# One decode step on one core: K and V loaded per head and batch in 6 KB runs, in place of both batches of a head in 12 KB runs

## The chip, the core and the metric

The kernel runs on one core of a Trainium2 chip. The core has five engines with an instruction stream each: TensorE (PE, matrix products; its weight loads are shown apart as PEld), VectorE (DVE), ScalarE (ACT), GpSimd (POOL) and SyncE (SP). Loads go from HBM to SBUF, the on-chip memory of 128 partitions, through 16 DMA engines; here SP issues every load. The metric is the device time of one execution in microseconds (us), the median of several runs.

## The reference

One token for each of two batches passes an attention block and a gated feed-forward block. The attention reads the last 2048 of 8192 cached positions of 32 heads, each 192 wide; all data are bfloat16.

```python
B, Sq, D = 2, 1, 640
Hq, Hkv, Sk, Dh = 32, 32, 8192, 192
W = min(4096, max(256, Sk // 4))                      # 2048
q = (x @ wq).reshape(B, Sq, Hq, Dh).transpose(0, 2, 1, 3)
k = k_cache[:, :, Sk - W:, :]
v = v_cache[:, :, Sk - W:, :]
p = softmax(einsum("bhqd,bhkd->bhqk", q, k) * Dh ** -0.5)
o = einsum("bhqk,bhkd->bhqd", p, v).transpose(0, 2, 1, 3).reshape(B, Sq, Hq * Dh) @ wo

h = x + A(layernorm(x))
h2 = h + (gelu(n @ w_gate) * (n @ w_up)) @ w_down     # n = layernorm(h)
```

K and V of the window are 2 x 32 x 2048 x 192 x 2 bytes each, 100.7 MB together; the weights add 21.6 MB.

## The kernel before

**Order.** The program is written once, operation by operation, through `P.op`, which notes what each operation reads (`R`), writes (`W`) and shares (`X`) and works out the semaphore waits. Each engine then runs its own operations in the order of writing. The heads are taken two at a time in 16 groups (`NG`), both batches together, so a group has four pairs of head and batch.

**The ring.** All loads go into one buffer, `ring`, of 110,592 bytes in each partition, at places handed out one after the other; where a load doesn't fit up to the end, it starts at 0 again. `load` queues a load, and `pump` issues queued loads in order on SP (L261). A load is put down only after the work that last read any earlier load in its place has been written (`done`), and its instruction waits for that work. Overlap is followed in steps of 256 bytes (`GRAN`). The loads' order: K of group 0, the first quarter of wq, K of group 1; then for each group K of the next group (and every fourth time a quarter of wq ahead of it), V of this group, and the group's rows of wo; at the end w_gate, w_up and three thirds of w_down. A load signals one of 32 semaphores in turn.

**K and V.** `kv_src` gives one head of both batches as 128 rows: row 2i is positions 32i to 32i+31 of batch 0, and row 2i+1 the same of batch 1. So one load puts 128 runs of 12,288 bytes into 128 partitions, batches on alternate partitions; there are 32 loads of K and 32 of V, 1536 KB each.

**Work on a group.** PE turns K over in blocks of 128x128 four-byte words (L427, 24 blocks a load, into four banks `tps`), and ACT (L436) and DVE (L439) copy the results into `ktr`, 1024 columns at a time. A four-byte word is a pair of neighbouring bf16 values, and since partitions alternate between batches, one kind of value lies at every fourth element of `ktr`. `q_stationary` (L468) makes the query columns with a `mask`; `scores` (L489) makes the scores of the four pairs in 24 products; `softmax` takes the maximum (L494 to L500) and the exponential (L502). The exponential writes every value twice, 1024 columns, since each of the columns goes to both batches' partitions. `e_columns` (L512) brings the exponentials into columns with eight small products, and a masked product on DVE with `bmask` (L316, as one of many) puts each into the columns of its own batch in `ering`. `pv` (L527) multiplies with V, 32 products a load. `o_columns` (L539, L541) and `oproj` (L556) of the group before make the output projection and add it to `hT`; this frees that group's wo.

**Order in a group's turn** g, on PE: first half of the transposes of group g+1; `e_columns(g)`; `o_columns(g-1)`; every fourth time the next query rows (L447); second half of the transposes; `oproj(g-1)`; `q_stationary(g+1)`; `pv(g)` for the first head; `scores(g+1)`; `pv(g)` for the second head; `softmax(g+1)`.

**The end.** After group 15: its output projection, the second layer norm, the gate and up products (L606), the activation, the down products (L629), the sum into `yT`, and the store (L637).

Of the kernel before, what the change touches and what calls it, by code (L numbers as in the profile page):

```python
# [143 lines left out]
KTP = 4  # L144
# [5 lines left out]
def bass_sequential_preLN__sliding_block_cached__geglu_ffn__decode_kernel(  # L150
# [11 lines left out]
):  # L162
    rep = 2
    with ExitStack() as ctx:
# [6 lines left out]
        def sb(name, shape, dt):  # L171
            return ctx.enter_context(nc.sbuf_tensor(name, shape, dt))
# [5 lines left out]
        ktr = sb("ktr", [128, KTP, 3, 2048], BF16)  # L178
# [10 lines left out]
        bmask = sb("bmask", [128, 2], F32)  # L189
        sel16 = sb("sel16", [128, 16], BF16)  # L190
# [27 lines left out]
        eexp = sb("eexp", [128, 1024], BF16)  # L218
        ering = sb("ering", [128, 2, 2, 32, 32], BF16)
# [48 lines left out]
        def kv_src(cache, q):  # L268

            return cache[:, q, SKT - WIN:, :].rearrange("b (i t) d -> i b (t d)", t=32)  # L270

        def load_k(g):
            for q in (2 * g, 2 * g + 1):
                load(("k", q), 2 * 32 * DH, kv_src(A_k_cache, q), lambda v: v)

        def load_v(g):
            for q in (2 * g, 2 * g + 1):
                load(("v", q), 2 * 32 * DH, kv_src(A_v_cache, q), lambda v: v)
# [55 lines left out]
        pool(lambda e: e.iota(ei[:, :], pattern=[[256, 3], [1, 2]], base=0, channel_multiplier=2), W=["ei"])  # L334
        pool(lambda e: e.memset(ering[:, :, :, :, :].rearrange("p a b c d -> p (a b c d)").bitcast(I32), 0), W=[("er", 0), ("er", 1)])
# [60 lines left out]
        dve(ts(oh_b[:, :], cf[:, 2, 31:33], pf[:, 5:6], ALU.is_equal, 0.5, ALU.mult), R=["cf2", "pf5"], W=["oh_b"])  # L396
        dve(ts(sel[:, :], cf[:, 0, 0:32:16], pf[:, 1:2], ALU.is_equal), R=["cf0", "pf1"], W=["sel"])
        dve(lambda e: e.tensor_copy(ef[:, :], ei[:, :]), R=["ei"], W=["ef"])
        for r in range(5):
            dve(ts(ge[:, :, r], ef[:, :], 192.0 * r, ALU.is_ge), R=["ef"], W=[("ge", r)])  # L400
        dve(tt(mask[:, :, :], ge[:, :, 0:4], ge[:, :, 1:5], ALU.subtract), R=[("ge", r) for r in range(5)], W=["mask"])

        dve(lambda e: e.tensor_copy(sel16[:, :].rearrange("p (j m) -> p j m", m=4),
                                    identf[:, :].rearrange("p (j m) -> p j m", m=32)[:, :, 0:4]), R=["identf"], W=["sel16"])

        dve(ts(pti[:, 0:1], pi[:, :], 1, ALU.bitwise_and), R=["pi", "pf1"], W=["pti0"])
        dve(lambda e: e.tensor_copy(pf[:, 6:7], pti[:, 0:1]), R=["pti0"], W=["pf6"])
        dve(ts(bmask[:, :], cf[:, 0, 0:2], pf[:, 6:7], ALU.is_equal), R=["cf0", "pf6"], W=["bmask"])
        mask_toks = ["mask"]

# [3 lines left out]
        def transposes(q):  # L414

            kk, ktoks = where["k", q]
            kv = kk.bitcast(F32)
            slot = q % KTP
            for bank in range(6):
                c, half = bank // 2, bank % 2  # L420
                bi = tb_count[0] % 4
                tb_count[0] += 1

                def fn(e, c=c, half=half, bi=bi):
                    for u in range(4):
                        off = 384 * (4 * half + u) + 128 * c
                        ins = e.transpose(tps[bi][:, 128 * u:128 * (u + 1)], kv[:, off:off + 128], identf[:, :])  # L427
                    return ins

                pe(fn, R=ktoks + ["identf"], X=[("t", bi)])  # L430
                if bank == 5:
                    done(("k", q))
                bv = tps[bi][:, :].bitcast(BF16)
                dst = ktr[:, slot, c, 1024 * half:1024 * (half + 1)]
                if bank in (2, 5) or (bank == 3 and q % 2 == 0):
                    act(lambda e, dst=dst, bv=bv: e.activation(out=dst, in_=bv, func=ACT.Copy),  # L436
                        W=[("kt", slot, bank)], X=[("t", bi)])
                else:
                    dve(lambda e, dst=dst, bv=bv: e.tensor_copy(dst, bv), W=[("kt", slot, bank)], X=[("t", bi)])  # L439
# [19 lines left out]
        def q_stationary(g):  # L459
            p0 = 32 * (g % 4)  # L460
            qx = qrow[p0:p0 + 2, (g // 4) % 2, :, 0:rep, :].rearrange("p h r d -> p h (r d)")

            def fn(e):
                for h in range(2):
                    for k in range(6):
                        col = 12 * h + 2 * k
                        o = 256 * (k // 2) % DH + k % 2
                        ins = e.matmul(m1[:, col:col + 2], lhsT=qx[:, h, o:o + 255:2],  # L468
                                       rhs=identb[p0:p0 + 2, p0:p0 + 2], start=True, stop=True, tile_position=(p0, 0))
                return ins  # L470

            pe(fn, R=[("qrow", (g // 4) % 2), "identb"], X=["m1"])
            for h in range(2):
                for b in range(2):
                    j = 2 * h + b
                    src = m1[:, 12 * h + b:12 * h + 12:2].unsqueeze(2).to_broadcast([128, 6, 4])
                    dve(tt(rq[:, g % 2, j, :, 0:4], src, mask[:, :, :], ALU.mult), R=mask_toks,
                        W=[("rq", g % 2)] if j == 0 else [("rq", g % 2, j)], X=["m1"])
# [4 lines left out]
        def scores(g):  # L483
            def fn(e):
                for k in range(6):
                    for j in range(4):
                        b = j % 2
                        r = ktr[:, (2 * g + j // 2) % KTP, k // 2, 2 * b + k % 2:2048:4]
                        ins = e.matmul(sps[32 * j:32 * (j + 1), :], lhsT=rq[:, g % 2, j, k, :], rhs=r, start=(k == 0),  # L489
                                       stop=(k == 5), tile_position=(0, 32 * j))  # L490
                return ins

            pe(fn, R=rq_toks(g) + [("kt", (2 * g + h) % KTP, x) for h in range(2) for x in range(6)], X=["s"])
            dve(lambda e: e.tensor_reduce(out=mx[:, :], in_=sps[:, :], axis=AX.X, op=ALU.max), W=["mx"], X=["s"])  # L494
            dve(ts(mrhs[:, :], oh_k[:, :], mx[:, 0:1], ALU.mult), R=["oh_k", "mx"], W=["mrhs"])

        def softmax(g):
# [4 lines left out]
            act(lambda e: e.activation(out=eexp[:, :].rearrange("p (x d) -> p x d", d=2),  # L502
                                       in_=sps[:, :].unsqueeze(2).to_broadcast([128, 512, 2]), func=ACT.Exp, bias=nm[:, 0:1], scale=1.0,
# [3 lines left out]
        def e_columns(g):  # L507

            def fn(e):
                for u in range(8):  # L510
                    o = m2[:, 0:128].rearrange("p (j t) -> p j t", t=32)[:, :, 4 * u:4 * u + 4]
                    ins = e.matmul(o, lhsT=eexp[:, 128 * u:128 * (u + 1)], rhs=sel16[:, :], start=True, stop=True)  # L512
                return ins

            pe(fn, R=["eexp", "sel16"], X=["m2"])
            src = m2[:, 0:128].rearrange("p (h b t) -> p h t b", h=2, b=2)
            dst = ering[:, g % 2, :, :, 0:32:16]
            dve(tt(dst, src, bmask[:, :].unsqueeze(1).unsqueeze(1).to_broadcast([128, 2, 32, 2]), ALU.mult), R=["bmask"],
                W=[("er", g % 2)], X=["m2"])

        def pv(g, h):
            vv, vtoks = where["v", 2 * g + h]

            def fn(e):
                for t in range(32):
                    r = t % 4
                    ins = e.matmul(ops_[32 * r:32 * (r + 1), 192 * h:192 * (h + 1)], lhsT=ering[:, g % 2, h, t, :],  # L527
                                   rhs=vv[:, DH * t:DH * (t + 1)], start=(h == 0 and t < 4), stop=(h == 1 and t >= 28),
                                   tile_position=(0, 32 * r), skip_group_check=True)
                return ins  # L530

            pe(fn, R=[("er", g % 2)] + vtoks, X=["o"])
            done(("v", 2 * g + h))
            if h == 1:
                act(lambda e: e.activation(out=osb[:, :], in_=ops_[:, 0:384], func=ACT.Copy), W=["osb"], X=["o"])  # L535
# [31 lines left out]
        transposes(0)  # L567
        transposes(1)
# [4 lines left out]
        for g in range(NG):  # L573
            nxt = g + 1 < NG
            if nxt:
                transposes(2 * g + 2)
            e_columns(g)
            if g > 0:
                o_columns(g - 1)
            if nxt and (g + 1) % 4 == 0:  # L580
                q_rows((g + 1) // 4)
            if nxt:
                transposes(2 * g + 3)
            if g > 0:
                oproj(g - 1)
            if nxt:
                q_stationary(g + 1)
            pv(g, 0)
            if nxt:
                scores(g + 1)  # L590
            pv(g, 1)
# [105 lines left out]
```

## Time and profile before

| | us |
|---|---|
| median of three runs | 305.15 (304.78 to 305.48) |
| the profiled execution | 305.48 |
| its span, first to last instruction | 303.6 |

| in the profiled execution | busy us | share of the span |
|---|---|---|
| PE, products | 235.6 | 78% |
| PEld, weight loads | 190.1 | 63% |
| DVE | 130.5 | 43% |
| ACT | 112.2 | 37% |
| load queue, mean of 16 DMA engines | | 96.9% |

The span is cut into 40 equal slices in the page, and each digit tells the busy share of a slice in tenths. "q1" is the queue of the loads that SP issues; its packets are the single contiguous runs and the small signals at a load's end. In a row of waits the columns are the engine and line that waited, what it waited for, the total, the number of times, and the longest, in us. A row of a group of instructions has the line, engine, operation, tiles and shapes, the count, the busy time in us and the mean of one in ns, and then the idle time ahead of it with what ended it. HBM was read at 403 GB/s over the span.

### The profile page before, as it was taken

How to read it: one execution, taken by the hardware profiler on the slowest of the kernel's cores; microseconds unless marked ns; L12 is line 12 of the kernel's file. 1: busy time of each engine (PE TensorE's matmuls, PEld its weight loads, DVE VectorE, ACT ScalarE, POOL GpSimd, SP SyncE). 2: the span in 40 equal slices, each digit the busy share in tenths (PEclk: the TensorE clock that was granted, in tenths of full speed). 3: DMA queues.
4: the chain of work that ended last, by engine and by line, in shares of the span. 5: the costliest groups of instructions: out<-in, count | busy, mean ns of one | idle time of the engine just before them, and what ended most of it. 6: DMA issues, size and time to landing. Idle time of an engine off the chain costs nothing.

```text
span 303.6 us, 7058 instructions
## 1 busy us (share of the span) xinstructions
PE 235.6 (78%) x3169; PEld 190.1 (63%) x3169; DVE 130.5 (43%) x360; ACT 112.2 (37%) x138; POOL 3.2 (1%) x9
## 2 busy tenths in 40 slices
PE   2878798962999988791898979692799889796762
PEld 1737394932868675771867676671785858575662
DVE  5837263720345364341446454351252736453120
ACT  2336343630425263522336353432243644442000
POOL 4000000000000000000000000000000000000000
PEclk9999979995798899798799999798579999998555
DMA  6999999999999999999999999999999999999980
GB/s 240 412 435 414 427 426 420 428 399 427 425 422 423 426 421 421 427 399 428 421 428 426 421 418 426 421 407 420 433 419 426 421 421 417 429 419 424 417 308 27
DMA packets 16323, 122.76 MB, mean 404 GB/s; under 512 B 1698, under 2 KB 3236, under 8 KB 7844
## 3 DMA queue, kind: packets, MB, share of 16 engines
q1 hardware_dynamic: 16292, 122.30, 96.9%
q8 instruction: 25, 0.41, 0.6%
q14 instruction: 6, 0.05, 0.0%
HBM read 122.29 MB, written 0.00 MB: 403 GB/s over the span
## 4 chain that ended last, share of the span: by engine, by line
DMA 57%; PE 31%; SPq 5%; DVE 3%; ACT 1%; issue 1%
DMA ring<-in_A_k_cache_dram 49%; PE tps L427 19%; DMA ring<-in_B_w_down_dram 8%; SPq L261 5%; PE m L541 3%; PE sps L489 3%; PE m L556 2%; PE ops L527 1%; ACT eexp L502 1%; PE m L447 1%; PE m L468 1%; PE m L539 1%; DVE mx L494 1%; DVE ktr L439 1%; PE m L512 1%
## 5 line engine op out<-in xcount | busy, mean ns | idle before, releaser
L427 PE MATMUL tps<-identf,ring 128*128 128x128 f32 x768 | 109.5, 305 | 37.4 <-DMA ring<-in_A_k_cache_dram 33.2
L427 PEld LDWEIGHTS tps<-identf,ring 128*128 128x128 f32 x768 | 101.1, 161 | 42.4 <-DMA ring<-in_A_k_cache_dram 34.0
L436 ACT ACTIVATE ktr<-tps 128x1024 bf16<-128x1024 bf16 x80 | 79.6, 1023 | 77.4 <-PE tps L427 77.4
L439 DVE COPY ktr<-tps 128x1024 bf16<-128x1024 bf16 x112 | 73.7, 688 | 47.3 <-PE tps L427 45.4
L489 PE MATMUL sps<-ktr,rq 128*32 128x512 bf16 x384 | 46.5, 631 | 0.7 <-DVE rq L316 0.5
L535 ACT ACTIVATE osb<-ops 128x384 f32<-128x384 f32 x16 | 7.9, 491 | 71.5 <-PE ops L527 71.5
L494 DVE TENSOR_REDUCE mx<-sps 128x1 f32<-128x512 f32 x16 | 11.1, 692 | 49.4 <-PE sps L489 49.4
L527 PEld LDWEIGHTS ops<-ring,ering 128*32 128x32 bf16 x1024 | 22.9, 101 | 10.5 <-issue 9.0
L527 PE MATMUL ops<-ring,ering 128*32 128x192 bf16 x1024 | 28.5, 255 | 0.2 <-DMA ring<-in_A_v_cache_dram 0.2
L489 PEld LDWEIGHTS sps<-ktr,rq 128*32 128x32 bf16 x384 | 10.9, 108 | 21.9 <-issue 21.0
L502 ACT ACTIVATE eexp<-sps,nm 128x1024 bf16<-128x1024 f32 x16 | 17.8, 1114 | 12.7 <-DVE nm L500 12.7
L541 PE MATMUL m<-sel,osb 128*128 128x2 f32 x96 | 19.4, 318 | 0.0
L541 PEld LDWEIGHTS m<-sel,osb 128*128 128x128 f32 x96 | 18.6, 269 | 0.0
L556 PEld LDWEIGHTS m<-ot,ring 128*128 128x128 bf16 x240 | 11.8, 129 | 1.1 <-DVE ot L316 1.1
L312 DVE TENSOR_SCALAR zrhs<-oh_b,zr 128x2 f32<-128x2 f32 x16 | 3.7, 229 | 20.4 <-ACT eexp L502 20.4
L556 PE MATMUL m<-ot,ring 128*128 128x2 bf16 x240 | 11.6, 177 | 0.9 <-DVE ot L316 0.9
L316 DVE TENSOR_TENSOR ering<-m,bmask 128x128 bf16<-128x128 f32 x16 | 11.3, 709 | 1.9 <-PE m L512 1.3
L498 PEld LDWEIGHTS m<-mrhs,pm 128*128 128x128 f32 x32 | 4.8, 188 | 11.5 <-DVE mrhs L312 11.5
L498 PE MATMUL m<-mrhs,pm 128*128 128x4 f32 x32 | 6.2, 263 | 7.1 <-DVE mrhs L312 7.1
L316 DVE TENSOR_TENSOR rq<-m,mask 128x24 bf16<-128x24 f32 x64 | 7.2, 175 | 9.6 <-PE m L468 9.6
L468 PE MATMUL m<-identb,qrow 2*128 2x2 bf16 x192 | 7.2, 159 | 4.6 <-DVE hT L316 3.7
L468 PEld LDWEIGHTS m<-identb,qrow 2*128 2x128 bf16 x192 | 5.8, 92 | 6.3 <-DVE hT L316 4.8
(84 smaller groups left out, 85.4 us busy)
## 6 DMA issues: line engine op xcount, KB each, us to landing
ring<-in_A_k_cache_dram SPq DMA_DIRECT2D x32, 1536.0 KB, 24.2
ring<-in_A_v_cache_dram SPq DMA_DIRECT2D x32, 1536.0 KB, 24.7
ring<-in_A_wq_dram SPq DMA_DIRECT2D x4, 1920.0 KB, 23.7
ring<-in_A_wo_dram SPq DMA_DIRECT2D x16, 480.0 KB, 19.7
ring<-in_B_w_gate_dram SPq DMA_DIRECT2D x1, 1920.0 KB, 27.4
ring<-in_B_w_up_dram SPq DMA_DIRECT2D x1, 1920.0 KB, 22.4
ring<-in_B_w_down_dram SPq DMA_DIRECT2D x3, 640.0 KB, 23.7
xrow<-in_A_x_dram SPq DMA_DIRECT2D x1, 2.5 KB
```

Source lines behind the costliest of these rows:

```text
L261: P.op("sp", lambda e, v=v, src=src: e.dma_start(v, src), W=toks + [("sem", i % NSEM)], dma=f"d{i % NSEM}")
L316: return lambda e: e.tensor_tensor(out=out, in0=a, in1=b, op=op)
L427: ins = e.transpose(tps[bi][:, 128 * u:128 * (u + 1)], kv[:, off:off + 128], identf[:, :])
L436: act(lambda e, dst=dst, bv=bv: e.activation(out=dst, in_=bv, func=ACT.Copy), W=[("kt", slot, bank)], X=[("t", bi)])
L439: dve(lambda e, dst=dst, bv=bv: e.tensor_copy(dst, bv), W=[("kt", slot, bank)], X=[("t", bi)])
L468: ins = e.matmul(m1[:, col:col + 2], lhsT=qx[:, h, o:o + 255:2], rhs=identb[p0:p0 + 2, p0:p0 + 2], start=True, stop=True, tile_position=(p ...
L489: ins = e.matmul(sps[32 * j:32 * (j + 1), :], lhsT=rq[:, g % 2, j, k, :], rhs=r, start=(k == 0), stop=(k == 5), tile_position=(0, 32 * j))
L494: dve(lambda e: e.tensor_reduce(out=mx[:, :], in_=sps[:, :], axis=AX.X, op=ALU.max), W=["mx"], X=["s"])
L502: act(lambda e: e.activation(out=eexp[:, :].rearrange("p (x d) -> p x d", d=2), in_=sps[:, :].unsqueeze(2).to_broadcast([128, 512, 2]), fu ...
L527: ins = e.matmul(ops_[32 * r:32 * (r + 1), 192 * h:192 * (h + 1)], lhsT=ering[:, g % 2, h, t, :], rhs=vv[:, DH * t:DH * (t + 1)], start=(h ...
L541: ins = e.matmul(m1[:, 32 + 2 * kk:34 + 2 * kk], lhsT=osb[:, kk:384:3], rhs=sel[:, :], start=True, stop=True)
L556: ins = e.matmul(m1[:, 48 + 2 * c:50 + 2 * c], lhsT=wo[:, kk, c:D:NC5], rhs=ot[:, kk, :], start=(kk == 0 and c == 0), stop=(kk == 2), skip ...
```

## The change

K and V are loaded for each head and batch alone. `kv_src(cache, n)` with n = 2 head + batch gives 128 rows of 16 positions, 6,144 bytes each and next to each other in HBM; there are 64 loads of K and 64 of V, 768 KB each. The places in the ring are in turn half as large, and come free one by one. The order of the bytes is otherwise kept. What follows from it in the work:

- `transposes(n)` handles one pair of head and batch in three banks of four blocks; a turn has four of them, and the other steps stand between them: one; `e_columns`; one; `o_columns`, query rows; one; `oproj`; one; `q_stationary`. `ktr` has 8 places of 1024 columns in place of 4 of 2048, and the scores read every second element.
- The exponential writes 512 columns. `e_columns` makes four 128x128 transposes in place of eight products, and a plain copy on DVE of 64 columns takes the place of the masked product; `bmask` and `sel16` go, and the factor 0.5 in `oh_b` with them. `ering` holds, for each pair, stationary columns shifted by batch.
- `pv(g, j)` runs for each of the four pairs, 16 products each: two ahead of the scores of the next group, two behind.
- A constant `LAYOUT`, set to "f32", chooses between two ways of turning K over; only the first is in the program that is built, and it is left out below where it has no effect.

```diff
-KTP = 4
+KTS = 8
...
-        ktr = sb("ktr", [128, KTP, 3, 2048], BF16)
+        ktr = sb("ktr", [128, KTS, 3, 1024], BF16)
...
-        eexp = sb("eexp", [128, 1024], BF16)
-        ering = sb("ering", [128, 2, 2, 32, 32], BF16)
+        eexp = sb("eexp", [128, 512], BF16)
+        ESTR = 528
+        ering = sb("ering", [128, 2, 4 * ESTR], BF16)
...
-        def kv_src(cache, q):
-
-            return cache[:, q, SKT - WIN:, :].rearrange("b (i t) d -> i b (t d)", t=32)
+        def kv_src(cache, n):
+            h, b = n // 2, n % 2
+            return cache[b, h, SKT - WIN:, :].rearrange("(p t) d -> p (t d)", p=128)
 
         def load_k(g):
-            for q in (2 * g, 2 * g + 1):
-                load(("k", q), 2 * 32 * DH, kv_src(A_k_cache, q), lambda v: v)
+            for n in range(4 * g, 4 * g + 4):
+                load(("k", n), 2 * T * DH, kv_src(A_k_cache, n), lambda v: v)
...
-        def transposes(q):
...
-            for bank in range(6):
-                c, half = bank // 2, bank % 2
+        def transposes(n):
+            for c in range(3):
...
-                        off = 384 * (4 * half + u) + 128 * c
+                            off = 384 * u + 128 * c
...
-                if bank == 5:
-                    done(("k", q))
+                if c == 2:
+                    done(("k", n))
...
-                if bank in (2, 5) or (bank == 3 and q % 2 == 0):
+                if c == 2 or (c == 1 and n % 4 == 1):
...
-                        r = ktr[:, (2 * g + j // 2) % KTP, k // 2, 2 * b + k % 2:2048:4]
+                            r = ktr[:, n % KTS, k // 2, :].rearrange("p (s e) -> p e s", e=2)[:, k % 2, :]
...
-            act(lambda e: e.activation(out=eexp[:, :].rearrange("p (x d) -> p x d", d=2),
-                                       in_=sps[:, :].unsqueeze(2).to_broadcast([128, 512, 2]), func=ACT.Exp, bias=nm[:, 0:1], scale=1.0,
+            act(lambda e: e.activation(out=eexp[:, :], in_=sps[:, :], func=ACT.Exp, bias=nm[:, 0:1], scale=1.0,
...
-                for u in range(8):
-                    o = m2[:, 0:128].rearrange("p (j t) -> p j t", t=32)[:, :, 4 * u:4 * u + 4]
-                    ins = e.matmul(o, lhsT=eexp[:, 128 * u:128 * (u + 1)], rhs=sel16[:, :], start=True, stop=True)
+                for cc in range(4):
+                    ins = e.transpose(ev[:, 128 * cc:128 * (cc + 1)], eexp[:, 128 * cc:128 * (cc + 1)], identb[:, :])
...
-            dve(tt(dst, src, bmask[:, :].unsqueeze(1).unsqueeze(1).to_broadcast([128, 2, 32, 2]), ALU.mult), R=["bmask"],
-                W=[("er", g % 2)], X=["m2"])
+            dve(lambda e: e.tensor_copy(dst, src), W=[("er", g % 2)], X=["m2"])
...
-        def pv(g, h):
-            vv, vtoks = where["v", 2 * g + h]
+        def pv(g, j):
+            n = 4 * g + j
...
-            done(("v", 2 * g + h))
-            if h == 1:
+            done(("v", n))
+            if j == 3:
...
             if nxt:
-                transposes(2 * g + 2)
+                transposes(4 * g + 4)
             e_columns(g)
+            if nxt:
+                transposes(4 * g + 5)
             if g > 0:
                 o_columns(g - 1)
             if nxt and (g + 1) % 4 == 0:
                 q_rows((g + 1) // 4)
             if nxt:
-                transposes(2 * g + 3)
+                transposes(4 * g + 6)
             if g > 0:
                 oproj(g - 1)
             if nxt:
+                transposes(4 * g + 7)
                 q_stationary(g + 1)
             pv(g, 0)
+            pv(g, 1)
             if nxt:
                 scores(g + 1)
-            pv(g, 1)
+            pv(g, 2)
+            pv(g, 3)
```

## The prediction

> **What bounds the kernel now.** I read the page's slices and DMA queue first, then stretches of single load kinds, then SP's waits, then the last 30 us. The page:
>
> ```profile
> span 303.6 us, 7058 instructions
> ...
> PE 235.6 (78%) x3169; PEld 190.1 (63%) x3169; DVE 130.5 (43%) x360; ACT 112.2 (37%) x138; POOL 3.2 (1%) x9
> ...
> DMA  6999999999999999999999999999999999999980
> ...
> q1 hardware_dynamic: 16292, 122.30, 96.9%
> ```
>
> The load queue keeps its 16 engines busy for 96.9% of the span: 0.969 x 303.6 = 294.2 us on each engine. The remaining 9.4 us are the start (the trace's first packet begins at 1.7 us) and the end (its last load packet ends at 297.4 us, 6.2 us ahead of the end of the span); between 8 and 281 us the packet records show only 1.3 us of idle time per engine. The busiest compute engine, PE, has 78%, and most of its idle time is a wait for K. So DMA time is the time.
>
> Next, the rate by size of packet. A packet is one contiguous run into one partition. In these stretches (DMA share and GB/s are the last two columns) the records hold 12 KB packets of K and V alone in the first three, 92% wq packets of 3072 B in the fourth, and in the last the down-projection's 1280 B packets:
>
> ```profile
> core 0: us, PE busy (x) PEld busy (x) DVE busy (x) ACT busy (x) POOL busy (x), PEclk, DMA share, GB/s
> 72.00:79.00 7.00, 4.72 (x22) 4.72 (x23) 1.54 (x3) 1.86 (x2) 0.00 (x0) 0.50 1.00 425
> 120.00:127.00 7.00, 4.31 (x45) 3.99 (x34) 2.55 (x6) 2.91 (x5) 0.00 (x0) 0.80 1.00 423
> ...
> 212.00:219.00 7.00, 4.37 (x21) 4.37 (x22) 1.38 (x2) 1.51 (x2) 0.00 (x0) 0.50 1.00 421
> ...
> 64.50:67.00 2.50, 1.74 (x42) 1.04 (x34) 1.08 (x3) 0.62 (x2) 0.00 (x0) 1.00 1.02 398
> ...
> 294.00:297.00 3.00, 2.27 (x56) 2.06 (x53) 0.51 (x3) 0.00 (x0) 0.00 (x0) 0.50 0.57 201
> ```
>
> The reader is to see that the queue is full in the first four rows and yet slower with small packets. The last row shows a share of 0.57: about half of the engines are done (in the records they end at 292 to 293 us), the others at 296 to 297. The end hangs on the later half.
>
> Then whether the queue ever runs dry:
>
> ```profile
> ring<-in_A_k_cache_dram SPq DMA_DIRECT2D x32, 1536.0 KB, 24.2
> ring<-in_A_v_cache_dram SPq DMA_DIRECT2D x32, 1536.0 KB, 24.7
> ```
> ```profile
> SPq L261 <- PE m L556: 140.1, 13, 20.8
> SPq L261 <- PE ops L527: 24.4, 12, 3.1
> ```
>
> A K load moves in 3.7 us (1.57 MB at 423 GB/s) but lands 24 us after its issue: it stands in line. SP's waits for ring places (the output projection's at L556 above all) are long, yet the bytes issued less the bytes landed never fall under 2.8 MB after the start (at 155.4 us), which is 6.6 us of transfer.
>
> **The change, part by part.**
>
> *Packets (L261).* Bytes stay the same. K and V go from 64 loads of 128 packets of 12,288 B to 128 loads of 128 packets of 6,144 B: 8192 packets become 16,384, or 512 more on each engine. The trace before has no 6 KB packet, so I bound its cost. From the stretches: 16 x 12288 / 423 = 464.8 ns a packet; the fourth row has a mean packet of 3,122 B, 16 x 3122 / 398 = 125.5 ns. The slope is (464.8 - 125.5) / 9166 = 0.0370 ns per byte, and 125.5 - 3122 x 0.0370 leaves 9.9 ns for every packet whatever its size. The records agree: mean durations of 57, 124, 151, 464 and 577 ns at 1280, 3072, 3840, 12,288 and 15,360 B (the slowest 0.5% left out) lie on one line. Split by rank, the quicker 7/16 of the packets of each size (as seven engines' worth) leave 7.8 ns and the slower 9/16 leave 11.8. The low end is the quick group, 512 x 7.8 = 4.0 us; the high end takes the slow tenth of the 3840 and 12,288 B packets (156 and 469 ns: 241.4 ns at 6144 B, 482.8 - 469 = 13.8 ns), 7.1 us. The later engines set the end, so I choose between all engines' 9.9 and the slow group's 11.8: 10.8 ns, 512 x 10.8 = **5.5 us**.
>
> *Completions.* 64 more loads each end in one 4-byte packet per engine, 9 ns in the records: 64 x 9 = **0.6 us**. Bounds: 0, if it lies beside the next packet, and 1.5 us, if each also takes as much idle time as the records show per load between packets (the 1.3 us above over 91 loads, 14 ns).
>
> *Issues on SP.* 64 more of some 0.55 to 0.6 us are 38 us, on an engine that waits over 200 us for places and for the end; each one feeds 786 KB, 1.9 us of transfer. Cost on the path **0**, hidden by the queued loads. One limit shows: some issues last up to 7.0 us in place of 0.54, when about 75 to 85 packets per engine stand unfinished. With 6 KB packets that limit is reached at half the bytes, but 75 x 0.238 = 18 us are then still queued, so SP is late and DMA is not. If this cover were gone, one 0.6 us issue per load would still be under 1.9 us.
>
> *Ring.* 12,288 is two times 6144, so all offsets, wraps and the order of the loads stay. Places come free in halves, and the output projection (which frees its weights) comes after three of four K pieces in place of all: some 1.9 us sooner. This can only lengthen the queue. **0**.
>
> *Waits on PE.* The transposes now wait for one 786 KB piece; behind each wait stand the exponent columns, the output columns and the projection, and behind those SP's next place. Each wait is for an earlier byte than before, so nothing is late by it.
>
> *Compute.* Transposes (768), K copies (80 on ACT, 112 on DVE, 1024 columns), score products (384) and value products (1024) keep their counts.
>
> ```profile
> L489 PE MATMUL sps<-ktr,rq 128*32 128x512 bf16 x384 | 46.5, 631 | 0.7 <-DVE rq L316 0.5
> ...
> L502 ACT ACTIVATE eexp<-sps,nm 128x1024 bf16<-128x1024 f32 x16 | 17.8, 1114 | 12.7 <-DVE nm L500 12.7
> ...
> L316 DVE TENSOR_TENSOR ering<-m,bmask 128x128 bf16<-128x128 f32 x16 | 11.3, 709 | 1.9 <-PE m L512 1.3
> ```
>
> The exponential writes 512 columns in place of 1024; nearest row is the 384-column copy on ACT, 491 ns, so about -0.5 us a group. The masked product of 128 columns becomes a copy of 64: between the 175 ns of a 24-column product and 709 ns, about -0.3 us. Eight small exponent matmuls (0.2 us together in the chain) become four 128x128 transposes, at most 4 x 305 ns by the K transposes' row: -0.2 to +1.0 us. The score products read every second element where they read every fourth: between no change and a gain. All of it, at most about 1 us a group either way, lies beside 18.4 us of DMA a group (294.2 / 16), with PE's 33 us of waits for K as cover: **0**. Were compute the bound, 16 groups would make -16 to +16 us of it.
>
> *The end.* The last load packet ends at 297.4, then a product, the sum and the store:
>
> ```profile
> 274.65 23.22 DMA ring<-in_B_w_down_dram
> 297.92 0.97 PE m L629 x20
> ```
>
> PE waits for the down-projection's weights, so the shorter value products ahead of it bring nothing; the 6.2 us stay.
>
> *Sum.* 5.5 + 0.6 = **+6.1 us**. The profiled run took 305.48 us with a span of 303.6 (1.9 us around it): it would become a span of 309.7 and a run of 311.6. That run is 0.3 above the median, 305.15, on which I put the forecast: **311.2 us**.
>
> *A rule against it.* The records and the queueing above price a load's end at 9 ns. The Trainium skill, "DMA: Bandwidth & Descriptors", Anatomy of one DMA, gives every DMA a fixed 2.0 us and its rules ask for at least 1 MiB each; 64 more loads would by that cost an estimated 128 us and end near 433 us. This trace doesn't bear that out: with 24 us in line, loads of 0.48 MB and 1.5 MB follow one another without a gap. The same page, Latency and other measured facts, tells of copies at half rate when partitions lie a large power of two apart; before, neighbouring partitions come from the two batches, 96 MiB apart, which would speak for a gain by contiguous loads. But the alternating 12 KB packets lie on the same line as the contiguous 15 KB ones (464 against 577 ns), so nothing is lost there now.
>
> **The rivals.**
>
> 1. *Contiguous reads pay* (faster). It would act in the reads of K and V and decides once two 6 KB packets take less than one of 12 KB, 467 ns in the mean of all, that is under 233 ns each. For it: the 12 KB stretches differ by 1% among themselves (421 to 425). Against: the straight line over five sizes, which holds both patterns. Were every 6 KB packet half of the quick group's 460 ns, 1024 x 230 = 235.5 us in place of 512 x 467 = 239.1 would save 3.6 us, less 0.6 for completions: 302.2 us.
>
> 2. *Packet cost hidden* (no change). If an engine overlaps a 6 KB packet's fixed part with the one before it, 0 to 0.6 us: 305.2 to 305.8. Against: 3072 and 3840 B packets don't hide it with a full queue.
>
> 3. *The queue runs dry* (slower still). If the packet limit or a late place leaves DMA idle where least was in flight, at the three wq groups, 2 us each on top: 317 us. For it: the limit above and 2.8 MB left at 155 us. Against: 6.6 us of cover there, and places that come free sooner.
>
> That the change doesn't do what it says can't well be: the run length follows from the source's layout.
>
> **How the numbers follow.** Forecast 0.85 (own range 309.0 to 313.0: +4.0 and no completion cost to +7.1 and 0.6), rival 1 0.06, rival 2 0.05, rival 3 0.04. The range reaches a little under the forecast's own, for rival 2's half-way cases, and over it for small gaps in the queue: 307.5 to 313.7. A change of 0.2% (0.6 us) is about what can be told from none. Slower 0.90, same 0.04, faster 0.06.
>
> **What would show it.** Some 24,500 packets on the load queue, 6 KB stretches at full DMA share with 16 x 6144 / 239 = 411 GB/s in place of 423, the share of the queue still near 97%, PE's waits for K longer, the exponential near 0.6 us. Wrong would be: 6 KB stretches at 423 or more; a DMA share under 0.98 between 20 and 285 us; or a last chain in which PE, not the down-projection's weights, ends last.

## The result and the profile after

The changed kernel takes 308.05 us (307.79 to 308.12, four runs) against 305.07 us for the kernel before (304.78 to 305.48): 1.0095 times the time, 95% interval 1.0078 to 1.0113, so 2.98 us slower. The forecast was 311.2 us. The direction and the kind of cost hold, and the time lies in the stated range, but the increase of 6.1 us was put about twice too large (1.6 to 1.7 times, against the repeat further down).

The page of the changed kernel, the lines that answer to those shown of before:

```profile
span 306.0 us, 7011 instructions
...
PE 226.7 (74%) x3105; PEld 196.4 (64%) x3105; DVE 125.9 (41%) x356; ACT 106.0 (35%) x138; POOL 3.3 (1%) x9
...
DMA  7999999999999999999999999999999999999982
...
q1 hardware_dynamic: 25508, 122.31, 98.2%
...
DMA 67%; PE 22%; SPq 8%; issue 1%; DVE 0%
```

PE, DVE and ACT are less busy, the load queue more: it carries 9216 packets more for the same 122.3 MB (8192 of data, 1024 of signals), and the share of loads in the chain that ended last (the last line) goes up. Before it was:

```profile
DMA 57%; PE 31%; SPq 5%; DVE 3%; ACT 1%; issue 1%
```

The stretches of time, with the same columns as before:

```profile
72.00:79.00 7.00, 5.93 (x36) 5.79 (x36) 2.68 (x5) 2.72 (x3) 0.00 (x0) 0.68 1.02 419
120.00:127.00 7.00, 4.65 (x38) 4.35 (x39) 2.21 (x5) 2.21 (x4) 0.00 (x0) 0.56 1.02 419
...
298.00:301.00 3.00, 2.40 (x64) 2.24 (x61) 0.18 (x1) 0.00 (x0) 0.00 (x0) 0.50 0.54 198
20.00:285.00 265.00, 203.78 (x2789) 176.26 (x2793) 110.55 (x290) 97.32 (x125) 0.00 (x0) 0.86 1.02 415
```

The middle of the span in the kernel before:

```profile
20.00:285.00 265.00, 214.73 (x2876) 172.08 (x2868) 114.61 (x290) 103.99 (x126) 0.00 (x0) 0.90 1.01 422
```

The queue is full, yet moves 419 GB/s where it moved 421 to 425, and 415 over the middle of the span where it moved 422. In the third row half of the engines are done, as before. The loads still land some 20 us after their issue, so the queue did not run dry:

```profile
ring<-in_A_k_cache_dram SPq DMA_DIRECT2D x64, 768.0 KB, 20.6
ring<-in_A_v_cache_dram SPq DMA_DIRECT2D x64, 768.0 KB, 20.3
```

The compute that the change shortens did get shorter, and nothing came of it:

```profile
L518 PE MATMUL sps<-ktr,rq 128*32 128x512 bf16 x384 | 25.0, 392 | 1.7 <-DVE rq L318 0.5
...
L531 ACT ACTIVATE eexp<-sps,nm 128x512 bf16<-128x512 f32 x16 | 11.0, 687 | 6.9 <-DVE nm L529 6.8
```

For what follows I cut the time at four points, from the packet records: when 3 MB have landed, when 118 MB have landed, the last load packet's end, and the end of the span. "Again" is a second profile of the two kernels, taken with the experiments; the medians below the first two rows stand beside 304.33 to 304.51 us for the kernel before in the same calls. A product of PE is two instructions.

| kernel | 3 MB at | 3 to 118 MB | 118 MB to last load | last load to end | median |
|---|---|---|---|---|---|
| before, first profile | 10.80 | 273.74 | 12.88 | 6.20 | 305.07 |
| after, first profile | 10.19 | 278.48 | 12.69 | 4.65 | 308.05 |
| before, again | 10.73 | 273.76 | 12.70 | 5.23 | 304.59 |
| after, again | 10.15 | 278.61 | 12.56 | 5.04 | 308.08 |
| old compute, 6 KB runs | 10.82 | 278.63 | 13.65 | 4.90 | 309.52 |
| new compute, half as many loads | 10.34 | 278.48 | 12.73 | 4.92 | 308.26 |
| new compute, 3 KB runs | 10.49 | 287.65 | 12.87 | 4.78 | 317.61 |
| after, alternating source | 10.81 | 278.51 | 12.69 | 5.09 | 308.77 |
| before, 1216 PE products left out | 10.78 | 273.10 | 12.04 | 4.86 | 302.72 |
| before, 576 PE products more | 10.85 | 274.23 | 13.68 | 4.93 | 305.48 |
| before, long down-projection runs | 10.77 | 273.77 | 12.36 | 8.90 | 307.02 |

### The profile page after: what moved, and what is told of

Its sections match the earlier page's. It is cut to its first block, busy times and chain, and to the rows that moved or that the text cites. A ratio compares the mean times of both kernels' runs of the same rounds, so it can differ in the third digit from the quotient of the medians.

```text
span 306.0 us, 7011 instructions
## 1 busy us (share of the span) xinstructions
PE 226.7 (74%) x3105; PEld 196.4 (64%) x3105; DVE 125.9 (41%) x356; ACT 106.0 (35%) x138; POOL 3.3 (1%) x9
## 4 chain that ended last, share of the span: by engine, by line
DMA 67%; PE 22%; SPq 8%; issue 1%; DVE 0%
DMA ring<-in_A_k_cache_dram 49%; PE tps L433 14%; DMA ring<-in_A_v_cache_dram 12%; SPq L263 8%; DMA ring<-in_B_w_down_dram 7%; PE m L575 2%; PE sps L518 2%; PE ops L560 1%; PE m L590 1%; PE m L540 1%; PE m L487 1%; PE m L668 0%; PE m L573 0%; SPq L320 0%; DVE yT L318 0%
## 5 line engine op out<-in xcount | busy, mean ns | idle before, releaser
L433 PE MATMUL tps<-identf,ring 128*128 128x128 f32 x768 | 121.9, 322 | 44.6 <-DMA ring<-in_A_k_cache_dram 42.4
L433 PEld LDWEIGHTS tps<-identf,ring 128*128 128x128 f32 x768 | 108.3, 171 | 48.0 <-DMA ring<-in_A_k_cache_dram 43.9
L560 PE MATMUL ops<-ring,ering 128*32 128x192 bf16 x1024 | 30.7, 254 | 12.4 <-DMA ring<-in_A_v_cache_dram 12.4
L518 PE MATMUL sps<-ktr,rq 128*32 128x512 bf16 x384 | 25.0, 392 | 1.7 <-DVE rq L318 0.5
L580 DVE RECIPROCAL rinv<-m 128x2 f32<-128x2 f32 x16 | 2.7, 171 | 32.0 <-PE m L575 32.0
L531 ACT ACTIVATE eexp<-sps,nm 128x512 bf16<-128x512 f32 x16 | 11.0, 687 | 6.9 <-DVE nm L529 6.8
L590 PEld LDWEIGHTS m<-ot,ring 128*128 128x128 bf16 x240 | 11.8, 129 | 1.1 <-DVE ot L318 1.1
L540 PE MATMUL m<-identb,eexp 128*128 128x128 bf16 x64 | 9.1, 290 | 1.2 <-ACT eexp L531 1.2
L547 DVE COPY ering<-m 128x64 bf16<-128x64 bf16 x16 | 7.0, 439 | 6.7 <-PE m L540 6.6
L529 DVE TENSOR_REDUCE nm<-m 128x1 f32<-128x4 f32 x16 | 2.6, 163 | 15.3 <-PE m L527 15.3
L540 PEld LDWEIGHTS m<-identb,eexp 128*128 128x128 bf16 x64 | 7.4, 139 | 2.0 <-DVE nm L529 1.2
```

What stands on the lines that cost most here:

```text
L531: act(lambda e: e.activation(out=eexp[:, :], in_=sps[:, :], func=ACT.Exp, bias=nm[:, 0:1], scale=1.0, accum_out=zr[:, 0:1]), R=["nm"], W=[ ...
L540: ins = e.transpose(ev[:, 128 * cc:128 * (cc + 1)], eexp[:, 128 * cc:128 * (cc + 1)], identb[:, :])
L560: ins = e.matmul(ops_[32 * r:32 * (r + 1), 192 * hh:192 * (hh + 1)], lhsT=ering[:, g % 2, col:col + 32], rhs=vv[:, DH * t:DH * (t + 1)], s ...
L590: ins = e.matmul(m1[:, 48 + 2 * c:50 + 2 * c], lhsT=wo[:, kk, c:D:NC5], rhs=ot[:, kk, :], start=(kk == 0 and c == 0), stop=(kk == 2), skip ...
```

## The experiments

My theory after the result (P): the extra packets alone cost the time, at 8 to 10 ns each. Rival L: the number of loads costs it. Rival C: the packets cost what the forecast said, and the new compute gave half back.

**Old compute, new traffic.** Each K and V load of the kernel before becomes two loads of 6 KB runs.

```diff
-            return cache[:, q, SKT - WIN:, :].rearrange("b (i t) d -> i b (t d)", t=32)
+            return cache[:, q, SKT - WIN:, :].rearrange("b (h i t) d -> h i b (t d)", h=2, t=16)
...
+                if key[0] in "kv":
+                    for j in range(2):
+                        P.op("sp", lambda e, v=v, src=src, j=j: e.dma_start(v[:, 3072 * j:3072 * (j + 1)], src[j]),
...
```

> The kernel before, with all its compute, but each K and V load put down as two loads of 6 KB runs (128 packets each): the traffic of the changed kernel under the compute of the old one. Theory P (the extra packets alone cost the time, some 8 to 10 ns each on every engine, and the new compute gives nothing): as the changed kernel, 307.5 to 308.5 us. Rival C (packets cost the forecast's 6.1 us and the finer waits and shorter compute gave 3 us back): 310.5 to 311.5 us.

Measured: 309.52 us (1.017, 1.0156 to 1.0184), between the two. The rate answers the question: 278.63 us from 3 to 118 MB, as with the new compute (278.48 and 278.61), so compute gave nothing back there, and C falls for this stretch. What is over sits at the two ends: 0.65 us at the start, and about 1.0 us between 118 MB and the last load; no run shows what the 1.0 us belongs to.

**Half as many loads.** The changed kernel with both batches of a head in one load of 256 packets.

```diff
...
+                    load((c + c, n), 4 * T * DH, cache[:, n // 2, SKT - WIN:, :].rearrange("b (p t) d -> p b (t d)", p=128),
+                         lambda v: v.rearrange("p (b x) -> p b x", b=2))
...
```

> The changed kernel, its compute and its 6 KB runs kept, but both batches of a head in one load of 256 packets: 64 loads of K and V in place of 128. Theory P: 307.7 to 308.7 us (completions save at most 0.6 us, and the larger first load gives back the 0.6 us by which the changed kernel's loads started ahead). Rival L (the number of loads costs, not the packets): back to 305.0 to 306.0 us.

Measured: 308.26 us, as P says. With 1024 signals fewer the rate is the same to 0.1 us (278.48): a load's completion costs nothing that shows here, and L falls.

**Still shorter runs.**

```diff
-            return cache[b, h, SKT - WIN:, :].rearrange("(p t) d -> p (t d)", p=128)
+            return cache[b, h, SKT - WIN:, :].rearrange("(f p t) d -> p f (t d)", f=2, p=128)
...
```

> The changed kernel with each K and V load as 256 packets of 3 KB (another order of positions within the window, the same for K and V): 1024 packets more on each engine, as many loads, the same compute. Theory P: 8.4 to 9.6 ns each, 8.6 to 9.8 us more, 316.6 to 317.9 us. At the forecast's 10.8 ns a packet: 319.1 us. Rival L: unchanged, 308 us.

Measured: 317.61 us (1.044, 1.0427 to 1.0453), within P's bounds. The middle of its span:

```profile
20.00:285.00 265.00, 196.53 (x2664) 169.07 (x2668) 108.77 (x286) 96.06 (x122) 0.00 (x0) 0.88 1.03 401
```

422, 415, 401 GB/s with 12, 6 and 3 KB, at a full queue each time. From 3 to 118 MB some 97.6 MB are K and V, 496 packets of 12 KB on each engine. The mean of the five kernels with 6 KB runs is 278.54 us, that of the two profiles of before 273.75: 4.79 / 496 = 9.7 ns for each packet more. The 3 KB runs add 9.11 us for 992 more: 9.2 ns. So the price of a packet is 9.2 to 9.7 ns.

**More loads, same packets.** Each K and V load of the kernel before as two loads of 64 partitions.

```diff
+                    for j in range(2):
+                        P.op("sp", lambda e, v=v, src=src, j=j: e.dma_start(v[64 * j:64 * j + 64, :], src[32 * j:32 * j + 32]),
...
```

> The kernel before with each K and V load put down as two loads of 64 partitions: 128 loads, but the same 8192 packets of 12 KB. Theory P: 304.7 to 305.8 us (0 to 0.6 us for the completions, up to 0.4 us saved at the start). Rival L: as the changed kernel, 308 us.

Measured: 510.21 us, the median of six runs between 505.78 and 533.58; by the four shorter ones 1.671 times the kernel before (1.6642 to 1.6775). Neither theory speaks of this, and as a test of the loads' number it is spoilt. Its page:

```profile
DMA packets 17347, 122.76 MB, mean 240 GB/s; under 512 B 2722, under 2 KB 4260, under 8 KB 8868
...
q1 hardware_dynamic: 17316, 122.31, 97.9%
```

The engines are as busy as ever and move little over half: a 12 KB packet lasts 823 ns in its records, 467 before. The Trainium skill, "SBUF — State Buffer", Door 1: The DMA port swizzle, says that bandwidth depends on how many of the 16 ports the partitions reach, and by its table partitions 0 to 63 reach eight. The 240 GB/s fit that; no run here varied the partitions in another way.

**Once more, side by side.** The two kernels as they are.

> The kernel before once more, for a second profile and to be timed beside the others on one chip. If the store at the end of the first profile (4.1 us from its issue to its landing) was a long one, the store takes some 2 to 3 us here and the span ends about 5 us after the last load packet, in place of 6.2. If it belongs to this kernel, 4 us again.

> The changed kernel once more, on the same chip as the others. Theory P (9.4 ns for each of 512 packets, nothing for the loads' number, 0.6 us gained at the start): the kernel before plus 3.5 to 4.4 us. Rival C (packets cost the 5.2 us of the 6 KB runs under the old compute, and the new compute gives 2 us back): plus 2.7 to 3.3 us, with a rate between 3 and 118 MB above that of the old compute.

Measured: 304.59 us (1.0006, 0.9998 to 1.0015) and 308.08 us (1.0123, 1.0110 to 1.0136), a difference of 3.5 us between the two and 3.7 against the 17 runs of before in that call. The store at the end:

```profile
out_dram<-yT SPq DMA_DIRECT2D x1, 2.5 KB, 2.8
```

So the 4.1 us of the first profile were a long store in that one execution, and the first profile of before is about 1 us too long at its end. The spans of the second pair differ by 3.94 us.

**Which engines end last.** I had put the later half of the DMA engines down to dearer packets. The time from the first packet's start to the last one's within a load (of the 16 loads of wo, all the same size, eight packets of 0.15 us for each engine; packet records) grows in steps: about 3.0 us up to 115 us, 4.6 from 131 us, 6.2 from 220 us, in the kernel before. PE's instructions come in 16 KB packets on the same engines (queue q8), 24 or 25 of them; the steps stand at the 9th and the 17th. Theory F: each holds up one of eight engines by 1.6 us, in turn. Two kernels change the number of PE's instructions. The first takes one of six score blocks and 4 of 32 value positions; the second makes the query products four times:

```diff
-                for t in range(32):
+                for t in range(4):
...
-                for k in range(6):
+                for k in range(1):
...
```
```diff
-                for h in range(2):
+                for h in (0, 1, 0, 1, 0, 1, 0, 1):
```

> The kernel before without most of the score and value products: scores take one of six blocks, value products 4 of 32 positions; loads are all there. 2432 PE instructions less. Theory F (the 16 KB instruction packets hold up eight of the DMA engines by some 1.6 us each, three times in turn, and so set the 4.3 us between the early and the late half): two rounds in place of three, the late half ends 1.6 us sooner, time 1.2 to 1.8 us under the kernel before, and the gap between the halves 1.6 us smaller. Rival (the late half is late by its data packets, and compute lies on no path): within 0.4 us of the kernel before, the same gap. If compute paced the loads at all: more than 2 us less, at a higher rate from 3 to 118 MB on both halves.

> The kernel before with the query products of each group made four times over, the same result: 1152 PE instructions more, some 1.35 us of PE a group, four or five more instruction packets. Theory F: a fourth round begins, the late half ends 1.6 us later, time 1.2 to 2.0 us above the kernel before. Rival (instruction packets don't matter, PE's extra work lies beside the loads): within 0.4 us of it.

Measured: 302.72 us (0.9946, 0.9934 to 0.9958) and 305.48 us (1.0047, 1.0031 to 1.0063). The instruction queue and the share of busy engines at the end, first with fewer instructions:

```profile
q8 instruction: 15, 0.25, 0.3%
```
```profile
294.00:297.00 3.00, 1.95 (x45) 1.79 (x44) 0.00 (x0) 0.00 (x0) 0.00 (x0) 0.50 0.30 108
```

Then before (again):

```profile
q8 instruction: 24, 0.39, 0.5%
```
```profile
294.00:297.00 3.00, 2.41 (x67) 2.29 (x65) 0.92 (x5) 0.22 (x1) 0.00 (x0) 0.50 0.56 200
296.00:299.00 3.00, 2.06 (x49) 1.93 (x47) 0.00 (x0) 0.00 (x0) 0.00 (x0) 0.50 0.16 56
```

And with more:

```profile
q8 instruction: 29, 0.48, 0.6%
```
```profile
296.00:299.00 3.00, 1.99 (x43) 1.76 (x40) 0.18 (x1) 0.00 (x0) 0.00 (x0) 0.50 0.36 130
```

15, 24 and 29 instruction packets; the later engines end sooner and later with them, and the gaps at the last wo load are 4.6, 6.3 and 7.5 us, one step of 1.2 to 1.7 us each. The steps move with the packets: with fewer instructions there is one, at the 9th packet (184 us); with more there are three, in the loads of wo at 115, 184 and 268 us, behind the 9th, 17th and 25th packet (104, 181 and 261 us). That is F: fewer by 1.65 us as expected, more by 1.1 us, a little under it. That the packets fall on eight engines is read from these steps; the records here do not name an engine. And 56 of the last wo load's 128 packets, seven engines' worth, start in the early group, so one engine more is late, and why stays open. The kernel with fewer products also has 14% less PE time, and its rate gains only 0.65 us in 274, about what nine instruction packets less make on the mean of 16 engines (9 x 1.6 / 16 = 0.9): compute paces nothing here.

**The start.** The changed kernel with the old kind of source, neighbouring partitions from two places.

```diff
-            return cache[b, h, SKT - WIN:, :].rearrange("(p t) d -> p (t d)", p=128)
+            return cache[b, h, SKT - WIN:, :].rearrange("(f i t) d -> i f (t d)", f=2, i=64)
```

> The changed kernel with neighbouring partitions from the two halves of the window (another order of positions, the same for K and V): 6 KB runs, 128 loads and the compute stay, only the source alternates as the old one's did. If the changed kernel's earlier start comes from its plain source pattern: SP's first issues take 0.6 us in place of 0.36, first K packets at 2.6 us in place of 2.2, and 0.4 to 0.7 us more than the changed kernel, the rate from 3 to 118 MB unchanged. If the alternation costs in the reading too, more. If the early start is due to the smaller loads: as the changed kernel.

Measured: 308.77 us, 0.7 above the changed kernel's 308.08, and the rate is the same (278.51). SP's first K issues, four loads each (start, length), in the changed kernel (again) and then here:

```profile
1.16 1.94 SPq L263 DMA_DIRECT2D ring<-in_A_k_cache_dram  x4
```
```profile
1.17 2.61 SPq L263 DMA_DIRECT2D ring<-in_A_k_cache_dram  x4
```

An issue of 0.64 us in place of 0.37 for the first load (records), and the first K packet at 2.75 us in place of 2.18. With old-style sources it is 2.57 to 2.75 in the seven profiles of such kernels with 128 partitions, with plain ones 2.15 to 2.22 in all four. So the early start belongs to the plain source, not to smaller loads. For a version with the first rows of wo loaded ahead of the first K, meant to shorten the old start, there is no time, so that stays open.

**A version that might beat both.** Packets cost time, so the kernel before with fewer of them in the down-projection:

```diff
-            wd = B_w_down.rearrange("(f p) n -> p f n", p=128)
+            wd = B_w_down.rearrange("(p f) n -> p f n", p=128)
...
-                        ins = e.matmul(bank[:, 2 * f:2 * f + 2], lhsT=wv[:, c, 128 * f:128 * (f + 1)], rhs=hnT[:, c, :],
+                        ins = e.matmul(bank[:, 2 * f:2 * f + 2], lhsT=wv[:, c, f:F:NF], rhs=hnT[:, c, :],
...
```

> The kernel before with the down-projection's weights in 128 runs of 5 KB a load in place of 512 of 1280 B (partition p takes hidden units 12p to 12p+11, and the gate and up products take every twelfth column to match): 72 packets less on each engine, nothing else. Theory P: 72 x 9.2 to 9.6 ns = 0.7 us less than the kernel before. If the packet cost is something of K and V alone: no change.

Measured: 307.02 us (1.0084, 1.0069 to 1.0100), slower; a miss. The last load does end sooner (296.9 us against 297.2), but by less than half of the 0.7 us expected, so no run here shows the price for other packets than those of K and V. And the span ends 8.9 us after it, not 5.2: the weight loads of the gate product, now with a step of 24 bytes, last 169 ns each where they lasted 104 (least, median, most, in ns; here and then before, again):

```profile
L606 PEld LDWEIGHTS sps<-hnT,ring x60: 138/169/186, 292.0 to 295.5; 128*128 128x128 bf16 x60
```
```profile
L606 PEld LDWEIGHTS sps<-hnT,ring x60: 103/104/115, 291.5 to 293.0; 128*128 128x128 bf16 x60
```

PE, which had waited for the down-projection's weights, now ends last. No version here beats the kernel before with all of its work done.

## Why the prediction was right and wrong

*Right.* The bound (the load queue), the direction, and the kind: more packets at a full queue. Also that, once the queue is full, issues on SP, the ring, the finer waits and the compute would cost and bring nothing: 3 to 118 MB take the same time with the old and the new compute. Rival 1 (contiguous reads pay) falls with the alternating source: the same rate. (96 MiB is not a power of two, so the page's row that the prediction named for this rival does not quite reach the case.) Rival 2 falls with the 3 KB runs. Rival 3 (the queue runs dry) didn't come: 20 us stay in line. That 308.05 us lies in the stated range is luck: it is under the forecast's own 309.0, and the range reached down there only for packet costs that are partly hidden, which the runs do not show. The mechanism held; the terms of the sum 5.5 + 0.6, and two that it put at nothing, had the wrong size.

*Packets: too dear.* The step that failed first is "so I choose between all engines' 9.9 and the slow group's 11.8: 10.8 ns". The runs show 9.2 to 9.7 ns, 4.7 to 4.95 us in place of 5.5. So the term was 0.55 to 0.8 us too large. The slow group does not stand for the later engines: those are late by the instruction packets that they carry, shown with 15, 24 and 29 of them, and their lag didn't change with 512 packets more (the gap at the last wo load is 6.4 us in both first profiles). The rates at full queue, which had given 9.9, were the better witness. Sums of packet durations mislead too: they rise by 6.4 us an engine, more than the time does, and the share of busy time rises from 1.01 to 1.02 and 1.03 with shorter packets, that is, records overlap. The 6 KB packet's record came out at the 239 ns put in the prediction, but the rate in the K and V stretches at 419 GB/s, not the 411 worked out from it.

*Completions: 0 in place of 0.6 us.* Half as many loads, the same rate. (The prediction priced the 1024 signals here but left them out of its "some 24,500 packets"; there are 25,508. The fixed 2.0 us per DMA that it named and set aside was fitted on loads that GpSimd issues; here SP issues them.)

*The start: -0.6 us, put at nothing.* I looked at how often SP issues, not at how long one issue takes ahead of the first packet.

*The end: -0.3 us; the prediction let its 6.2 us stay.* Between 118 MB and the last load 0.15 to 0.2 us less, and behind it 0.2 us less in the second pair.

Together, by the second pair's rows, 4.85 - 0.58 - 0.14 - 0.19 = 3.94 us. This is the difference of the two spans, cut at three points, so it shows where the time lies and does not prove the causes. Of the 6.1 us forecast, 2.2 us are thus accounted for. The first comparison gave 2.98, with a 95% interval of 2.4 to 3.4 us that doesn't reach the 3.7 of the second. In it the kernel before took 305.07 us, in the later calls 304.33 to 304.59, while the changed kernel took the same in both: what is missing between 2.98 and the repeat lies in the kernel before and not in the change. The long store explains the one profiled run of the four; why the others were longer too stays open (the record does not say on which chip they ran). So does the 1.0 us at the end of the old compute with 6 KB runs: its engines spread further (7.7 us at the last wo load, 6.4 in the changed kernel), already by 0.7 us at 30 us, and no run took that apart.

## What to carry to other kernels

With a full load queue, price a change in run length from the rates of stretches with one size of packet each, and take the price per byte and the price per packet from those; don't add up packet durations or split them by rank. Then look at the two ends apart from the middle: what the first issue costs ahead of the first packet, and which engines end last and why. A shorter path on engines that wait for loads brings nothing, and a cheaper load that makes the last products slower loses.

## What the runs showed of the hardware

- PE's own instructions are loads too: 16 KB packets, as the steps tell in turn on eight of the 16 DMA engines, each putting its engine back by about 1.6 us (its own record lasts 1.07 us; what makes up the rest no run shows). 2432 PE instructions less made this kernel 1.65 us shorter. The Trainium skill, "Runtime: NRT & Kernel Launch", Instruction fetch mechanics, tells of 16 KiB blocks by a queue of the engine's own and calls the cost mostly hidden; where the data queue is the bound, these runs show it on the path.
- A source that alternates between two places made one issue on SP last 0.64 us in place of 0.37, though its packets are no slower.
- With K and V loaded into 64 partitions at a time the span's mean was 240 GB/s with all engines busy, with 128 partitions 406 (before, again).
- The score products went from 631 to 392 ns each with their moving columns read in steps of 4 bytes in place of 8; their shapes stayed the same.
